# Moving output-projection halves around each context tile, summing the last blocks in PSUM, and reordering the loads and the start of an attention-times-FFN kernel

## The chip, the cores and the metric

The kernel runs on one core of one Trainium2 chip. Times are device microseconds of that core. Unless a profile is named, a time is the median of four to seven executions. Engines are called by their usual short names: PE is TensorE, DVE is VectorE, ACT is ScalarE, POOL is GpSimd, and SP is SyncE, which here only issues DMAs.

## The reference

With x of shape 2048 x 640 and 32 heads of 192 columns, cut to what matters:

```python
xn = layernorm(x)
k, v = k_cache[:, :, 1536:], v_cache[:, :, 1536:]      # the last 512 keys only
p  = softmax((xn @ wq) @ k.T * 192 ** -0.5)            # per head
s  = (p @ v, heads side by side) @ wo                  # 6144 -> 640
g  = silu((silu(xn @ w_gate) * (xn @ w_up)) @ w_down)
out = x + s * g
```

## The kernel before

The kernel has a head (layer norm and feed-forward, giving g), then 64 attention steps: 16 pairs of heads by 4 blocks of 512 queries. Step `i` computes the scores of `i`, the query projection of `i+1`, the context (`pv`) of `i-1` and the output projection (`wo_half`) of `i-3`. Everything is issued in program order on every engine. The result of `wo_half` is added on DVE to `sacc`, in SBUF, for 16 tiles of 128 queries. DVE also prepares the keys of the next pair: it sums them (the K sums) and subtracts their mean. Two PSUM accumulators named `mm` serve both the query chunks and the output halves. The cuts are marked with "...".

```python
def mm_tile():                                   # two buffers for q chunks and output halves
    return psum.tile([P, 512], f32, name="mm", tag="mm", bufs=2)

def q_chunk(i, j):
    q_ps = mm_tile()
    ...                                          # 5 matmuls of 512 columns
    nc.scalar.copy(qTs[i][:, j, :], q_ps[:, :])  # ACT frees the buffer

def wo_half(i, qt, n):
    ps = mm_tile()
    ...                                          # 3 matmuls of 320 columns
    nc.vector.tensor_tensor(sacc[:, t, cols], sacc[:, t, cols], ps[:, 0:HD], ALU.add)
    if pr == NPAIR - 2 and n == 1:
        pre_final(t)                             # POOL: sacc = sacc * g2 + x
    ...                                          # last pair: DVE or ACT+POOL make ob, SP stores it

order = ("A", 0, 1, "q0", 2, 3, "B", 4, "q1", 5, 6, "q2", 7)
for step in order:                               # A, B: scores; q: query chunk
    ...
        wo_half(i - LAG, step // 2, step % 2)    # one half, then one context half
        pv(i - 1, step // 2, step % 2)
        prepare_pair(i, step)                    # loads, K transposes, K sums of the next pair
```

In the head all gate, up and down weights are issued before the x tiles 4 to 7, all on SP except the first quarter of the up weights, which ACT issues.

The softmax here doesn't subtract the row's maximum and nothing guards it: scores larger than these inputs give would overflow.

## Time and profile before

| | before |
|---|---|
| median of the first four runs | 1005.62 us |
| span of the profiled run | 1003.2 us |
| PE busy | 974.6 us (97%) |
| start to first exponential of step 0 | 185.2 us |
| from there to first exponential of step 63 | 772.5 us |
| from there to the end | 45.5 us |

The last three rows come from the starts of ACT's exponentials in the timeline. They split the span into head, steady part and tail. A PE that is 97% busy can still be losing time: the profile draws each group of matmuls to its modelled end, which overlaps the start of the next group, so short holes show only as a late start of the next one. Therefore look at starts.

From the page of the kernel before: the span, PE's busy time, and the clock granted to TensorE in 40 slices (tenths of full speed).

```profile
span 1003.2 us, 16007 instructions
...
PE 974.6 (97%) x6540; PEld 564.7 (56%) x6540; DVE 522.7 (52%) x1265; ACT 421.1 (42%) x561; POOL 151.5 (15%) x188
...
PEclk8999999999999999999999999999999999999979
```

**Steady.** From the timeline of the kernel before, PE alone (start, duration, engine, line, operation, output and inputs, count; in brackets, where there are any, the idle time before and what ended it), and DVE alone and one line of ACT in the same stretch:

```profile
504.77 0.50 PE L373 MATMUL pv<-V_b_210,p_t 128*128 128x193 bf16 x4
505.20 0.57 PE L412 MATMUL mm<-wo_p,OT_b 128*128 128x320 bf16 x3
...
505.94 1.24 PE L158 MATMUL mm<-xnT,wq_p 128*128 128x512 bf16 x5
507.17 0.57 PE L412 MATMUL mm<-wo_p,OT_b 128*128 128x320 bf16 x3
...
507.91 1.02 PE L347 MATMUL sc<-qT,khat 128*128 128x512 bf16 x4
...
520.33 1.03 PE L347 MATMUL sc<-qT,khat 128*128 128x512 bf16 x4
```

```profile
506.05 0.68 DVE L140 TENSOR_REDUCE ssum<-KT 128x1 f32<-128x512 bf16 x1
506.64 0.48 DVE L419 TENSOR_TENSOR sacc<-sacc,mm 128x320 f32<-128x320 f32 x1
```

```profile
504.56 0.59 ACT L163 CAST qT<-mm 128x512 bf16<-128x512 f32 x1
```

Four context matmuls (pv) take 0.33 us from start to next start elsewhere, but the output half after those at 504.77 starts 0.43 us later, at 505.20, just when ACT's eviction of the query chunk has ended (504.56 to 505.15). The half at 507.17 starts 1.23 us after the query chunk at 505.94, which takes 1.07 us where nothing is in the way. It starts 50 ns after the add at 506.64 ends, and that add stood behind a K sum. The two score groups (L347) at 507.91 and 520.33 begin two steps.

A step takes 12.42 us, and 12.57 us in the third block of each pair, where the K sums are.

**Head.** The same view, around the wait for x tile 4:

```profile
23.21 0.89 DVE L207 BATCH_NORM_STATS2 stats<-x_t 128x6 f32<-128x320 bf16 x2 [5.82 <-DMA x_t<-in_A_x_dram]
24.13 0.21 DVE L208 BATCH_NORM_AGGREGATE mv<-stats 128x2 f32<-128x12 f32 x1
24.26 0.64 DVE L257 TENSOR_TENSOR hT<-sc,sg 128x512 bf16<-128x512 f32 x1
...
24.95 2.29 PE L251 MATMUL sc<-xnT,wg_sb 128*128 128x512 bf16 x5 [4.60 <-DVE hT L257]
```

DVE works in order. The statistics of x tile 4 wait for a load queued behind all weights, the product hT is behind them, and PE waits for hT. The five matmuls at 24.95 then take 2.29 us where they take 1.24 us at full clock.

**Tail.** Who PE waited for after 955 us (total, times, longest), from the timeline two output additions on DVE with POOL's work beside the first, and the line of the windows view for 970 to 980 us (busy time and count by engine, then the granted clock, the DMA share and GB/s):

```profile
PE mm L412 <- DVE s_f L431: 11.1, 15, 1.7
```

```profile
959.80 1.41 POOL L403 TENSOR_TENSOR sacc<-sacc,g_76 128x640 f32<-128x640 f32 x1
...
960.04 1.53 DVE L432 TENSOR_TENSOR ob<-s_f,sacc 128x320 bf16<-128x320 f32 x1
...
976.29 0.49 DVE L432 TENSOR_TENSOR ob<-s_f,sacc 128x320 bf16<-128x320 f32 x1
```

```profile
970.00:980.00 10.00, 7.98 (x42) 5.37 (x42) 9.52 (x20) 0.00 (x0) 4.72 (x4) 0.59 0.41 105
```

The same addition took 1.53 us beside POOL's multiplication and 0.49 us alone. The Trainium skill, page "SBUF — State Buffer", section "SBUF: two separate sides", says that a DVE operation with two SBUF inputs and a GpSimd operation that reads SBUF exclude each other on a shared pair of ports, each for a whole instruction. The trace agrees: the slow addition ends 0.36 us after POOL's multiplication (961.57 and 961.21). In the window from 970 to 980 us PE was also granted only 0.59 of full speed.

### The profile page before, as it was taken

Reading aid. Unit: us, or ns where it says so; the run is one execution under the profiler, and the core shown is the slowest. Engines: PE = TensorE matmul, PEld = TensorE weight load, DVE = VectorE, ACT = ScalarE, POOL = GpSimd, SP = SyncE. Lnnn points to the kernel's source line nnn. Section 1 sums busy time; section 2 is a strip of 40 time slices with the busy share of each in tenths; the row PEclk is TensorE's granted clock in tenths of the full one; section 3 lists DMA queues with packets and bytes.
Section 4 is the critical chain, followed back from the end, with each engine's and each line's share of the span. In section 5 each row is a group of like instructions: output and inputs, shape, how many; then the busy total and the mean of one; then the engine's idle time right before and its main releaser. Section 6 shows DMA issues by size and latency. Waiting matters only on the chain. (4 is left out here: it accounts for less than half of the span.)

```text
span 1003.2 us, 16007 instructions
## 1 busy us (share of the span) xinstructions
PE 974.6 (97%) x6540; PEld 564.7 (56%) x6540; DVE 522.7 (52%) x1265; ACT 421.1 (42%) x561; POOL 151.5 (15%) x188
## 2 busy tenths in 40 slices
PE   6999999999999999999999999999999999999974
PEld 2455555555555555555555555555555555555553
DVE  3443411155555565656555655555555555556585
ACT  2332322554444444444444444444444444444421
POOL 1020400000101010101010101010101010005875
PEclk8999999999999999999999999999999999999979
DMA  9040800033533333324333423343433233222332
GB/s 301 27 99 2 157 17 1 1 59 73 87 64 87 64 88 64 88 63 87 65 87 63 88 63 88 64 87 64 87 64 88 63 87 65 58 49 55 74 97 73
DMA packets 145593, 74.18 MB, mean 74 GB/s; under 512 B 127856, under 2 KB 138608, under 8 KB 145520
## 3 DMA queue, kind: packets, MB, share of 16 engines
q1 hardware_dynamic: 135872, 41.40, 20.8%
q0 software_dynamic: 8704, 30.94, 12.1%
q8 instruction: 51, 0.84, 0.3%
q10 hardware_dynamic: 944, 0.82, 0.3%
q14 instruction: 22, 0.18, 0.1%
HBM read 39.45 MB, written 2.62 MB: 42 GB/s over the span
## 5 line engine op out<-in xcount | busy, mean ns | idle before, releaser
L419 DVE TENSOR_TENSOR sacc<-sacc,mm 128x320 f32<-128x320 f32 x448 | 217.6, 486 | 294.4 <-PE mm L412 291.7
L360 ACT ACTIVATE p_t<-sc 128x1024 bf16<-128x1024 f32 x256 | 248.1, 1020 | 229.9 <-PE sc L355 229.8
L412 PE MATMUL mm<-wo_p,OT_b 128*128 128x320 bf16 x1536 | 293.9, 301 | 11.5 <-DVE s_f L431 11.1
L158 PE MATMUL mm<-xnT,wq_p 128*128 128x512 bf16 x960 | 238.2, 379 | 0.0
L412 PEld LDWEIGHTS <-OT_b 128*128 128x128 bf16 x1536 | 139.0, 97 | 144.9 <-issue 69.8
L373 PEld LDWEIGHTS <-p_t 128*128 128x128 bf16 x2048 | 186.1, 98 | 42.1 <-issue 1.7
L163 ACT CAST qT<-mm 128x512 bf16<-128x512 f32 x192 | 112.3, 585 | 192.9 <-PE mm L158 184.4
L382 DVE TENSOR_TENSOR O_b<-pv,r 128x384 bf16<-128x384 f32 x256 | 142.7, 557 | 8.8
L347 PE MATMUL sc<-qT,khat 128*128 128x512 bf16 x512 | 131.8, 379 | 1.1 <-ACT qT L163 0.9
L158 PEld LDWEIGHTS <-wq_p 128*128 128x128 bf16 x960 | 90.7, 97 | 69.3 <-issue 0.8
L373 PE MATMUL pv<-V_b_210,p_t 128*128 128x193 bf16 x768 | 96.2, 249 | 0.0
L257 DVE TENSOR_TENSOR hT<-sc,sg 128x512 bf16<-128x512 f32 x48 | 33.1, 689 | 96.1 <-ACT sg L256 96.1
L373 PE MATMUL pv<-V_b_214,p_t 128*128 128x193 bf16 x640 | 79.5, 246 | 0.0
L373 PE MATMUL pv<-V_b_212,p_t 128*128 128x193 bf16 x640 | 79.5, 246 | 0.0
L355 PE MATMUL sc<-qT,khat 64*128 64x512 bf16 x512 | 77.5, 381 | 0.0
L251 PE MATMUL sc<-xnT,wg_sb 128*128 128x512 bf16 x240 | 61.6, 389 | 5.4 <-DVE hT L257 4.6
L347 PEld LDWEIGHTS <-khat 128*128 128x128 bf16 x512 | 48.1, 97 | 32.4 <-issue 2.0
L256 ACT ACTIVATE sg<-sc 128x512 bf16<-128x512 f32 x48 | 28.7, 597 | 86.4 <-PE sc L251 86.4
L251 PE MATMUL sc<-xnT,wu_sb 128*128 128x512 bf16 x240 | 61.6, 389 | 0.0
L381 DVE RECIPROCAL r<-pv 128x2 f32<-128x2 f32 x256 | 41.5, 162 | 34.9 <-PE pv L373 34.9
L119 POOL DMA_DIRECT2D wo_p<-in_A_wo_dram x16 | 12.3, 769 | 310.8 <-PE mm L412 310.8
L265 PE MATMUL mm<-wd_sb,hT 128*128 128x320 bf16 x384 | 56.6, 299 | 0.0
(55 smaller groups left out, 423.6 us busy)
## 6 DMA issues: line engine op xcount, KB each, us to landing
wq_p<-in_A_wq_dram POOLq DMA_DIRECT2D x16, 480.0 KB, 7.0
wo_p<-in_A_wo_dram POOLq DMA_DIRECT2D x16, 480.0 KB, 4.4
K_p<-in_A_k_cache_dram POOLq DMA_DIRECT2D x32, 192.0 KB, 4.3
x_r<-in_A_x_dram POOLq DMA_DIRECT2D x16, 160.0 KB, 2.6
out_dram<-ob SPq DMA_DIRECT2D x16, 160.0 KB, 1.8
V_b_210<-in_A_v_cache_dram POOLq DMA_DIRECT2D x12, 192.0 KB, 3.1
x_t<-in_A_x_dram SPq DMA_DIRECT2D x14, 160.0 KB, 4.1
wg_sb<-in_B_w_gate_dram SPq DMA_DIRECT2D x4, 480.0 KB, 8.3
```

The source lines that it names most:

```text
L158: nc.tensor.matmul(q_ps[:, :], pairs[pr]["wq"][:, c, j * P : (j + 1) * P], xnT[:, c, b * 512 : (b + 1) * 512], start=(c == 0), stop=(c == ...
L163: nc.scalar.copy(qTs[i][:, j, :], q_ps[:, :])
L251: nc.tensor.matmul(gu[:, s, :], w_sb[:, c, f * P : (f + 1) * P], xnT[:, c, qc], start=(c == 0), stop=(c == NC - 1),)
L265: nc.tensor.matmul(dn[:, 0:HD], hTs[b][:, f, ti * P : (ti + 1) * P], wd_sb[:, f, cols], start=(f == 0), stop=(f == NF - 1),)
L347: nc.tensor.matmul(sc[:, h, :], khat[:, 2 * h, ks], qT[:, 2 * h, :], start=True, stop=False)
L355: nc.tensor.matmul(sc[:, h, :], khat[r, 1, ks], qT[r, 1, :], start=False, stop=True)
L360: nc.scalar.activation(p_t[:, :, :], sc[:, :, :], ACT.Exp, scale=scale)
L373: nc.tensor.matmul(acc[:, h, 0 : Dh + 1], Ps[i][kc][:, h, qt * P : (qt + 1) * P], V_p[:, kc, h, 0 : Dh + 1], start=(kc == 0), stop=(kc == ...
L381: nc.vector.reciprocal(r[:], acc[:, :, Dh : Dh + 1])
L382: nc.vector.tensor_tensor(Obs[i][:, qt, :, :], acc[:, :, 0:Dh], r[:].to_broadcast([P, 2, Dh]), ALU.mult)
L412: nc.tensor.matmul(ps[:, 0:HD], OTs[i][:, 3 * qt + j, :], pairs[pr]["wo"][:, j, cols], start=(j == 0), stop=(j == 2),)
L419: nc.vector.tensor_tensor(sacc[:, t, cols], sacc[:, t, cols], ps[:, 0:HD], ALU.add)
```

## The change

The intent is threefold. In the steady part, the two output halves of a tile stand around both context halves, so that an `mm` buffer has time to come free. In the head, x tiles 4 to 7 are loaded between the weights and PE is kept busy. In the tail, blocks 2 and 3 of the last two pairs are summed in PSUM at the end, and the output of those tiles is made by DVE alone; POOL's multiply-and-add for them comes earlier, after pair 13 (pairs count from 0), and for the tiles of blocks 0 and 1 it now comes last. Some buffer counts change too. The diff, cut to its core:

```diff
 # head
-load all of w_gate, w_up, w_down, then x tiles 4-7
+load w_gate/w_up quarters 0, 1; x tiles 4-7; quarters 2, 3; w_down
+keep_warm(13) ... keep_warm(9) ... keep_warm(1) ...     # matmuls on zeros between the transposes
-if nx and f < 4: ln_stats(...)
+if nx and 2 <= f < 6: ln_stats(...)
-ln_apply partly on ACT
+ln_apply on DVE throughout
 # steady
-order = ("A", 0, 1, "q0", 2, 3, "B", 4, "q1", 5, 6, "q2", 7)
+order = ("A", 0, "q0", 1, "B", 2, "q1", "q2", 3)
-wo_half(i - LAG, step // 2, step % 2); pv(i - 1, step // 2, step % 2)
+wo_half(o, step, 0); pv(i - 1, step, 0); pv(i - 1, step, 1); wo_half(o, step, 1)
-K sums at context halves 1, 3, 5
+K sums at "q0", "B", "q1"
 # tail
+def load_xr(t):
+    xrs[t] = finp.tile([P, D], bf, name="x_r", bufs=4)
+    nc.sync.dma_start(out=xrs[t][:], in_=x2[t * P : (t + 1) * P, :])       # was on nc.gpsimd
+def gate_and_add(t, dst):                                                # POOL, two operations
+    nc.gpsimd.tensor_tensor(sacc[:, t, :], sacc[:, t, :], g2[:, t, :], ALU.mult)
+    nc.gpsimd.tensor_tensor(dst, sacc[:, t, :], xrs.pop(t)[:], ALU.add)
+def store(t, ob):
+    nc.sync.dma_start(out=out2[t * P : (t + 1) * P, :], in_=ob[:])
+wo_half, last pair, blocks 0 and 1: n == 0: load_xr(t); n == 1: gate_and_add(t, ob), store(t, ob)
+wo_late(b, qt): 12 matmuls of pairs 14 and 15 into PSUM; DVE: s_f = ps * g2, ob = s_f + sacc; store
+the last context blocks are transposed by DMA on nc.sync, one tile of 128 queries at a time
+the very last block is scaled on ACT (was DVE); PE transposes it, as before
```

## The prediction

> **What bounds the kernel.** TensorE (PE): the page gives a span of 1003.2 us with PE busy 974.6 us (97%). By the starts of matmuls in the timeline, a 512-column matmul takes a slot of 213 ns, a 320-column one 133, a 193-column one 80, and two 64-row score matmuls share a slot. All columns at that rate are an estimated 900 us. The other 103 us are gaps; the change is about three groups of them.
>
> 1. *Steady attention* (58 of 64 steps of pair and query block). A step takes 12.42 us, 12.57 us in the one of four with K's sums, for 11.53 us of columns. The timeline shows about 0.3 us of holes per step before output halves (16.1 us between 220 and 900 us): there are two "mm" accumulators, and a half waits for the 585 ns query eviction on ScalarE, or for the 486 ns sacc add behind a 675 ns K sum on VectorE. Another 0.3 us per step stands around the 64-row matmuls.
> 2. *Head.* PE idles 4.6 us at 20.4-25.0 us: VectorE, in order, stands at the statistics of x tile 4, whose load is behind all weights (landing at 23.2 us). Matmuls at 12.0-15.6 and 25.0-29.2 us have twice the spacing (427 ns). PE loses 9.0 us between 12 and 40 us.
> 3. *Tail.* After 960 us there are 17.6 us of columns and 18.7 us of gaps: output halves wait for VectorE's s_f/ob (0.48 + up to 1.53 us while GpSimd runs), later for GpSimd's s_f/ob, 1.8 us per tile (chain of waits). The granted clock (windows view) falls to 0.59 at 970-980 us.
>
> **What the change does, costed.**
> - Steady: the output halves stand around both context halves (0.67 us), so the half after a query chunk comes 1.07 us after it; eviction takes 0.8. The tight spot becomes reciprocal, 557 ns O_b scaling, then sacc add: the buffer is free 2.15 us after the context tile starts, and PE wants it at 2.145. Nearly no hole, no margin. K's sums move to slack. Expect 12.15 us per step: minus 16 us.
> - Head: x tiles 4-7 come after half of the weights, statistics start two hidden blocks later; extra zero matmuls keep the clock up. The Trainium skill ("TensorE: Matmul & The Clock Gate", Part 1) says the clock halves after an idle window of about 3.4 us and needs as long to return; the doubled spacings agree. Hidden blocks start near 11.3 instead of 12.03 us, at full rate: minus 9.3 us.
> - Tail: 8 tiles of the last two pairs accumulate in PSUM, without GpSimd or ScalarE in the output; a 640-column pair of VectorE operations (estimated 1.7 us from 486 ns per 320) faces 1.6 to 2.4 us of PE per tile. Gaps fall from 18.7 to about 2.5 us, the end after the last matmul from 6.9 to 6.2: minus 17 us.
>
> PE is critical throughout, so the parts add: minus 42 us, span 961.5 us, time **963.5 us**, 80% range **956 to 972**. Faster by over 2%: 0.97; within 2%: 0.025; slower: 0.005.
>
> **What would show it.** Steps of 12.1 to 12.2 us, the same for all four blocks; no PE gap over 1 us after 12 us; no granted clock under 0.95 after the first hidden block; 427 ns spacing only in the first zero matmuls; after the last step about 17 us of dense PE work, GpSimd's gate-and-add (2.8 us per tile) finishing under it.
>
> **What would make it wrong.** The sacc wait showing 0.1 us twice per step (+10 us); weights landing later than hidden blocks need them; the in-order SyncE queue holding the last transposes behind stores that wait for GpSimd; VectorE's ob slowed by GpSimd (1.53 against 0.49 us).

## The result

The changed kernel took 972.42 us (972.38 to 973.19, four runs) against 1005.62 us before. The ratio is 0.9671, with a 95% interval of 0.9654 to 0.9688. A ratio is the mean time of one kernel's runs over that of the other's of the same rounds, so not quite the ratio of the medians. It is faster by 3.3%, but the gain is 33 us and not 42, and 972.42 is just outside the predicted 956 to 972.

From the page after, the same lines:

```profile
span 970.6 us, 15644 instructions
...
PE 945.9 (97%) x6449; PEld 561.5 (58%) x6550; DVE 507.5 (52%) x1233; ACT 419.7 (43%) x559; POOL 127.5 (13%) x152
...
PEclk9999999999999999999999999999999999999999
```

Some matmul records are missing (6449 of 6550), so groups below sometimes count one short.

**Steady after**, from the timeline, PE alone and DVE alone:

```profile
503.59 1.03 PE L355 MATMUL sc<-qT,khat 128*128 128x512 bf16 x4
...
506.17 0.57 PE L438 MATMUL mm<-wo_p,OT_b 128*128 128x320 bf16 x3
506.58 1.24 PE L158 MATMUL mm<-xnT,wq_p 128*128 128x512 bf16 x4
507.66 0.57 PE L438 MATMUL mm<-wo_p,OT_b 128*128 128x320 bf16 x3
...
515.77 1.03 PE L355 MATMUL sc<-qT,khat 128*128 128x512 bf16 x3
```

```profile
506.58 0.56 DVE L392 TENSOR_TENSOR O_b<-pv,r 128x384 bf16<-128x384 f32 x1
507.05 0.48 DVE L456 TENSOR_TENSOR sacc<-sacc,mm 128x320 f32<-128x320 f32 x1
```

The add that frees the buffer ends at 507.53 and the next half starts at 507.66, 1.08 us after the query chunk began, so there is no hole. The step, from the score group at 503.59 to that at 515.77, takes 12.18 us, the median in all four blocks.

**Head after.** The hidden blocks start at 11.09 us at full clock, and the statistics of x tile 4 wait for nothing:

```profile
11.09 1.24 PE L254 MATMUL sc<-xnT,wg_sb 128*128 128x512 bf16 x4 [0.24 <-DVE xnT L245]
...
19.00 0.87 DVE L218 BATCH_NORM_STATS2 stats<-x_t 128x6 f32<-128x320 bf16 x2
```

**Tail after.** Here is what had not been expected. Who PE waited for after 925 us:

```profile
PE pv L381 <- ACT O_b L397: 4.9, 2, 3.1
PE sc L438 <- DMA OT_b<-O_b: 3.5, 2, 1.8
PE trp L416 <- ACT O_b L397: 1.5, 1, 1.5
PE mm L438 <- DMA OT_b<-O_b: 0.6, 1, 0.6
```

These waits sum to 10.5 us. PE waited for transposed context tiles (OT_b), and for ACT's scaling of the last block, which waited for a reciprocal on DVE. DVE, in turn, stood before that reciprocal at an addition whose output buffer `ob` was not yet stored:

```profile
DVE ob L485 <- DMA out_dram<-ob: 7.6, 2, 4.8
```

SP's and POOL's timelines in the same stretch:

```profile
937.55 0.34 SPq L428 DMA_DIRECT2D out_dram<-ob  x1
937.94 0.42 SPq L421 DMA_DIRECT2D x_r<-in_A_x_dram  x1
938.47 1.18 SPq L401 DMA_TRANSPOSE OT_b<-O_b  x1
941.79 0.34 SPq L428 DMA_DIRECT2D out_dram<-ob  x1
```

```profile
931.67 1.40 POOL L425 TENSOR_TENSOR ob<-sacc,x_r 128x640 bf16<-128x640 f32 x1 [2.71 <-DMA x_r<-in_A_x_dram]
...
937.48 1.40 POOL L424 TENSOR_TENSOR sacc<-sacc,g_76 128x640 f32<-128x640 f32 x1
940.37 1.40 POOL L425 TENSOR_TENSOR ob<-sacc,x_r 128x640 bf16<-128x640 f32 x1 [1.49 <-issue]
```

Read them as one circle. The store at 941.79 waits for POOL's addition, which runs from 940.37 to 941.77. That addition waits for the x_r load issued at 937.94. The load was issued only after the store of the tile before, at 937.55, and that store had waited for POOL's previous addition. The profile itself names the load as what ended the wait only at 926.20 and 931.67; at 940.37 it prints "issue", which names nothing. That the load is the cause there too is shown by e1 and e4 below, which change only the loads. So one tile takes 4.2 us here and 4.57 us on average (the first addition starts at 921.70 and the eighth at 953.72, seven periods), where POOL's own work is 2.8 us. The context transpose at 938.47 is in the same queue, and it too is held to this beat.

The parts of the span, from ACT's exponentials in the timelines (us):

| | to step 0 | steps 0 to 63 | step 63 to end | time |
|---|---|---|---|---|
| before | 185.2 | 772.5 | 45.5 | 1005.6 |
| after | 175.7 | 754.0 | 40.8 | 972.4 |

Step 61 of the changed kernel has no output halves and takes 8.92 us instead of 12.18; those 3.3 us of work are done in the tail. With them put back, the spans say: head 9.5 us, steady 15.2, tail 7.9 us saved, 32.6 in all.

### The profile page after: what moved, and what is told of

It reads as the page before. It is cut to its first block, busy times and chain, and to the rows that moved or that the text cites. A ratio compares the mean times of both kernels' runs of the same rounds, so it can differ in the third digit from the quotient of the medians.

```text
span 970.6 us, 15644 instructions
## 1 busy us (share of the span) xinstructions
PE 945.9 (97%) x6449; PEld 561.5 (58%) x6550; DVE 507.5 (52%) x1233; ACT 419.7 (43%) x559; POOL 127.5 (13%) x152
## 3 DMA queue, kind: packets, MB, share of 16 engines
q0 software_dynamic: 7936, 28.32, 11.3%
## 4 chain that ended last, share of the span: by engine, by line
PE 91%; DMA 2%; issue 2%; DVE 2%; POOL 1%; SPq 0%; ACT 0%; POOLq 0%; DVEq 0%
PE mm L158 21%; PE mm L438 21%; PE pv L381 17%; PE sc L355 11%; PE sc L254 10%; PE sc L363 7%; PE mm L268 5%; DMA x_r<-in_A_x_dram 1%; POOL ob L425 1%; DMA KT<-K_p 0%; PE tp L240 0%; DVE stats L218 0%; DVE s_f L482 0%; DMA out_dram<-ob 0%; DMA x_t<-in_A_x_dram 0%
## 5 line engine op out<-in xcount | busy, mean ns | idle before, releaser
L438 PE MATMUL mm<-wo_p,OT_b 128*128 128x320 bf16 x1452 | 276.6, 300 | 1.3 <-DVE sacc L456 0.7
L158 PE MATMUL mm<-xnT,wq_p 128*128 128x512 bf16 x915 | 225.7, 379 | 2.8 <-DVE sacc L456 0.4
L438 PEld LDWEIGHTS <-OT_b 128*128 128x128 bf16 x1536 | 136.2, 97 | 106.4 <-issue 51.9
L381 PEld LDWEIGHTS <-p_t 128*128 128x128 bf16 x2048 | 177.8, 97 | 27.5 <-issue 3.9
L158 PEld LDWEIGHTS <-wq_p 128*128 128x128 bf16 x960 | 93.7, 98 | 93.4 <-issue 1.5
L392 DVE TENSOR_TENSOR O_b<-pv,r 128x384 bf16<-128x384 f32 x252 | 140.5, 558 | 8.8 <-DVE r L390 0.3
L355 PE MATMUL sc<-qT,khat 128*128 128x512 bf16 x472 | 129.4, 379 | 3.0 <-ACT qT L163 0.9
L381 PE MATMUL pv<-V_b_222,p_t 128*128 128x193 bf16 x768 | 79.8, 246 | 4.9 <-ACT O_b L397 4.9
L381 PE MATMUL pv<-V_b_226,p_t 128*128 128x193 bf16 x640 | 66.5, 246 | 0.0
L381 PE MATMUL pv<-V_b_224,p_t 128*128 128x193 bf16 x640 | 66.5, 246 | 0.0
L254 PE MATMUL sc<-xnT,wg_sb 128*128 128x512 bf16 x230 | 59.1, 379 | 0.8 <-DVE xnT L245 0.2
L254 PE MATMUL sc<-xnT,wu_sb 128*128 128x512 bf16 x234 | 58.5, 379 | 0.2
```

The lines of the kernel that those rows point to most:

```text
L158: nc.tensor.matmul(q_ps[:, :], pairs[pr]["wq"][:, c, j * P : (j + 1) * P], xnT[:, c, b * 512 : (b + 1) * 512], start=(c == 0), stop=(c == ...
L254: nc.tensor.matmul(gu[:, s, :], w_sb[:, c, f * P : (f + 1) * P], xnT[:, c, qc], start=(c == 0), stop=(c == NC - 1),)
L355: nc.tensor.matmul(sc[:, h, :], khat[:, 2 * h, ks], qT[:, 2 * h, :], start=True, stop=False)
L381: nc.tensor.matmul(acc[:, h, 0 : Dh + 1], Ps[i][kc][:, h, qt * P : (qt + 1) * P], V_p[:, kc, h, 0 : Dh + 1], start=(kc == 0), stop=(kc == ...
L392: nc.vector.tensor_tensor(O_b[:, qt, :, :], acc[:, :, 0:Dh], r[:].to_broadcast([P, 2, Dh]), ALU.mult)
L438: nc.tensor.matmul(ps, OTs[i][:, 3 * qt + j, :], pairs[i // NB]["wo"][:, j, cols], start=(first and j == 0), stop=(last and j == 2),)
```

## The experiments

Three theories went into the first round. The ring theory says that the missing gain is the circle just shown. Rival 1 says that POOL's eight tiles are simply too much work for the shortened last steps. Rival 2 says that three `ob` buffers are too few. Two further runs ask whether the head and the order have the gains credited to them. All kernels gave correct results.

### e1_xr_act: the x_r loads on another queue

```diff
-nc.sync.dma_start(out=xrs[t][:], in_=x2[...])
+nc.scalar.dma_start(out=xrs[t][:], in_=x2[...])
```

> One line differs from the changed kernel: the loads of x for the final addition (x_r) are issued by ScalarE's queue instead of SyncE's. Ring theory (the changed kernel's tail is slow because, on the in-order SyncE queue, the x_r load of a tile stands behind the store of the tile before, that store waits for GpSimd's addition, and GpSimd's addition waits for the x_r load, so GpSimd goes at 4.4 us per tile and holds the context transposes and stores behind it): the loads land early, GpSimd goes at 2.8 us per tile, PE's waits for OT_b after 935 us vanish, time 963 to 966 us against 972.4. Rival 1 (GpSimd's 8 gate-and-add tiles are simply too much work for the last two steps): within 1 us of 972.4. Rival 2 (three ob buffers are too few): 970 or more.

Measured: 963.87 us (963.57 to 964.55), ratio to the kernel before 0.9595. POOL's additions now follow each other in 3.06 us on average (922.68 to 944.11, seven periods; 2.8 had been expected). PE's waits after 925 us:

```profile
PE trp L416 <- ACT O_b L397: 1.1, 1, 1.1
PE pv L381 <- ACT O_b L397: 0.4, 1, 0.4
```

No wait for OT_b is left. Rival 1 falls: POOL's work is the same and 8.5 us are back. What remains of a buffer shortage is one DVE wait of 2.8 us for an `ob` buffer.

### e2_ob8: more output buffers alone

```diff
-ob = finp.tile([P, D], bf, name="ob")
+ob = finp.tile([P, D], bf, name="ob", bufs=8)
```

> The changed kernel with 8 output buffers (ob) instead of 3, nothing else. Ring theory: PE's three waits for OT_b (0.6, 1.8 and 1.7 us) stay and two more come in their place; only VectorE's waits for an ob buffer go; GpSimd keeps 4.4 us per tile; time 969 to 971.5 us. Rival 2 (buffers are the cause): 963 to 966 us. Rival 1 (GpSimd's work): about 972.

Measured: 971.43 us (971.02 to 974.0), ratio 0.9675, so no different from the changed kernel at 0.9671, and within what the ring theory expected. PE's waits after 925 us:

```profile
PE sc L438 <- DMA OT_b<-O_b: 6.9, 4, 2.1
PE mm L438 <- DMA OT_b<-O_b: 1.0, 1, 1.0
```

The waits behind DVE went, and waits for the transposes took their place: five, as expected. POOL's additions came no faster than before (4.83 us apart on average). Rival 2 falls as the main cause. The buffer waits were a second effect of the same late stores, lying in the shadow of the late transposes.

### e4_xr_early: the same queue, loads four tiles ahead

```diff
+if i == NS - LAG:                       # the step without output halves
+    for t in range(4): load_xr(t)
 # wo_half, last pair, after store(t, ob):
+    if b == 0: load_xr(t + 4)
-if n == 0 and (pre or final): load_xr(t)
+if n == 0 and pre: load_xr(t)
```

> The changed kernel with the x_r loads still on SyncE's queue, but issued four tiles ahead (the first four in the step without output halves, each of the others after the store of the tile four before). Ring theory: the ring is broken though the queue is the same: GpSimd at 2.8 us per tile, 963 to 966 us, as with the loads on ScalarE's queue (963.9). If instead it was the load on SyncE's queue as such (a load between two transposes delaying them): 970 or more.

Measured: 962.74 us (962.62 to 963.1), ratio 0.9575, a little under the expected 963 to 966. The loads stay on SP, and the circle is cut by their place in the queue alone. POOL's timeline:

```profile
935.70 1.40 POOL L424 TENSOR_TENSOR sacc<-sacc,g 128x640 f32<-128x640 f32 x1
937.18 1.40 POOL L425 TENSOR_TENSOR ob<-sacc,x_r 128x640 bf16<-128x640 f32 x1
```

There is no bracket before the addition: the load has long landed. PE's waits after 925 us fall from 10.5 to 1.0 us (0.6 and 0.4, both for ACT).

### e3_store_pool: POOL issues the stores of its own tiles

```diff
-store(t, ob)                            # SP
+store(t, ob, nc.gpsimd)                 # for the eight gate-and-add tiles
```

> The changed kernel with the stores of the eight gate-and-add tiles issued by GpSimd itself; x_r loads and transposes stay on SyncE as they were. Ring theory: SyncE no longer waits for GpSimd except for an x_r buffer four tiles back, so loads and transposes go early; GpSimd pays about 0.6 us more per tile for issuing (3.4 us per tile): 964 to 967 us. If the three ob buffers or GpSimd's work were the cause: 971 or more.

Measured: 968.09 us (967.72 to 968.24), ratio 0.9627. The expectation of 964 to 967 was missed. SP's loads and transposes did go early, with no PE wait for OT_b, but POOL went at 3.80 us per tile and not 3.4, and one wait of another kind was left. POOL's timeline, then PE's only wait after 925 us, then DVE's:

```profile
936.85 1.40 POOL L425 TENSOR_TENSOR ob<-sacc,x_r 128x640 bf16<-128x640 f32 x1
938.55 0.58 POOL L428 DMA_DIRECT2D out_dram<-ob  x1 [0.30 <-POOL ob L425]
```

```profile
PE pv L381 <- ACT O_b L397: 5.2, 1, 5.2
```

```profile
DVE ob L485 <- DMA out_dram<-ob: 5.0, 2, 4.0
```

Issuing a store costs POOL 0.58 us and another 0.30 us until it sees its own addition done. At that pace the third `ob` buffer does come back too late, and PE waits behind DVE. After that wait the granted clock was 0.50 from 945 to 950 us (windows view), so this miss has a second part that the waits do not show.

### e6_store_pool_ob8: the same with eight buffers

> GpSimd issues the stores of its eight tiles (968.1 us, a miss: 964 to 967 was expected), now with 8 ob buffers. Its profile shows GpSimd at 3.8 us per tile and one PE wait of 5.2 us behind VectorE, which waits 4.0 us for an ob buffer. If that buffer wait is the whole of the miss: 962.5 to 964.5 us and no PE wait over 1 us in the tail. If GpSimd's slower pace costs otherwise: 966 or more.

Measured: 963.29 us (963.26 to 963.71), ratio 0.9586, as expected from the buffer wait. One PE wait of 1.4 us stayed, where none over 1 us had been expected. So the miss of the run before was the buffers (with the clock lost in the wait they caused). Whether they matter depends on how late the stores are.

### p_order and p_head: parts of the change on the kernel before

p_order is the kernel before with the new order of the step and the new places in it for K's loads, transposes, sums and centring, and nothing else. p_head is the kernel before with the new head alone.

```diff
 # p_order
-order = ("A", 0, 1, "q0", 2, 3, "B", 4, "q1", 5, 6, "q2", 7)
+order = ("A", 0, "q0", 1, "B", 2, "q1", "q2", 3)   # wo_half, pv, pv, wo_half in each tile
 # p_head
-head of the kernel before
+head of the changed kernel
```

> The kernel before with the order of the step alone: output halves around both context halves, chunks q1 and q2 together, K's sums beside the chunks; head and tail as before. If the two output halves' waits for the mm accumulators are the 0.3 us holes: steps of 12.18 us in all four blocks, about 14 us less than before, 990 to 993 us. If instead the shorter steps of the changed kernel come from another part of it (buffer counts, fewer GpSimd and DMA issues), steps stay near 12.42 us.

> The kernel before with the head of the changed one alone (x tiles 4-7 between the weights, later statistics, zero matmuls, VectorE for all normalisations). If the head's gain is its own: first exponential at 175.7 us as in the changed kernel (185.2 before), 9 to 10 us less than before, 995.5 to 997 us, steps of 12.42 and 12.57 us unchanged.

Measured: p_order 989.99 us (988.62 to 991.59), ratio 0.9855; p_head 996.43 us (996.38 to 996.52), ratio 0.9918. p_order's steps take 12.18 us, and its part from step 0 to 63 is 755.9 us against 772.5. p_head reaches step 0 at 175.9 us against 185.2, and its steps keep 12.42 and 12.57 us. Both 95% intervals lie below 1 (0.9837 to 0.9872, and 0.9901 to 0.9935). Each part brings its own gain; p_order does not touch the head, nor p_head the steps.

### p_head_order: the changed kernel without its tail

```diff
-tail of the changed kernel
+tail of the kernel before, with the new head and the new order
```

> The changed kernel without its tail: the kernel before with the new head and the new step order. If the parts add: 1005.6 - 9.2 - 15.6 = 981 us, so that the tail as it is brings 8 to 9 us (predicted 17), and with the ring broken 17. If head and order interact, this run differs from 981 by more than 2 us.

Measured: 980.48 us (980.08 to 981.08), ratio 0.9751. The parts add within 2 us: against the kernel before in their own rounds (1004.95 us) they bring 15.0 and 8.5 us, and together, against 1005.64 us, 25.2. (The expected 981 us had mixed rounds.) From here to the changed kernel are 8.1 us, and to e4_xr_early 17.7 us: that is what this tail brings with the ring and without it.

### e5_xr_act_ob8 and e7_best: both repairs

```diff
+e5: x_r loads on ACT's queue, ob bufs=8
+e7: x_r loads four tiles ahead on SP, ob bufs=8
```

> Both: x_r loads on ScalarE's queue and 8 ob buffers. With the ring gone the profile still shows VectorE waiting 2.8 us for an ob buffer and PE 1.5 us behind it. If that wait is real: 962 to 963 us; if GpSimd's stores still pace the end: 963.9 as without the buffers.

> x_r loads four tiles ahead on SyncE and 8 ob buffers: the two repairs that each took waits out of the tail. VectorE still waited 2.3 us for an ob buffer with the early loads alone, PE some 0.6 us behind it. Expected 961.5 to 962.7 us against 962.7 without the buffers; if the buffers do nothing here, 962.7 within 0.3.

Measured: e5 963.04 us (962.82 to 963.19), ratio 0.9577, just above what was expected. e7 took 961.93 us (961.71 to 962.06), ratio 0.9573 (0.9558 to 0.9587). Its only PE wait after 925 us:

```profile
PE pv L381 <- ACT O_b L397: 0.4, 1, 0.4
```

e7 beats both kernels. It is 0.8 us under e4 by the medians, but the two ran in different rounds, and by the ratios (0.9575 and 0.9573) the difference is 0.2 us. One wait of 0.6 us vanished from the profile; a gain from the buffers here is not shown by the times.

The spans of all runs, from ACT's exponentials (us):

| | to step 0 | steps 0 to 63 | step 63 to end |
|---|---|---|---|
| before | 185.2 | 772.5 | 45.5 |
| p_head | 175.9 | 772.5 | 46.3 |
| p_order | 185.7 | 755.9 | 46.7 |
| p_head_order | 175.9 | 756.9 | 45.6 |
| after | 175.7 | 754.0 | 40.8 |
| e2_ob8 | 175.8 | 754.1 | 39.8 |
| e3_store_pool | 175.9 | 753.8 | 36.7 |
| e6_store_pool_ob8 | 175.9 | 754.5 | 31.5 |
| e1_xr_act | 176.0 | 754.8 | 31.2 |
| e4_xr_early | 175.9 | 754.2 | 30.8 |
| e5_xr_act_ob8 | 175.9 | 755.0 | 30.3 |
| e7_best | 176.1 | 753.8 | 30.0 |

Only the last column moves among the variants of the tail. The middle column varies by about 1 us even where nothing in it was changed. In the changed kernel one step of 13.53 us accounts for 1.35 us: a K transpose issued at 676.32 landed 4.58 us later, where the median is 2.7 us, and DVE stood behind it. It is step 42, and in the profiles that same step takes 13.3 to 13.6 us in all nine runs that have both the new head and the new order, and 12.2 to 12.6 us in the other three (e1 and e5 have one more, step 58, of 13.1 and 13.2 us). So it is not random: it comes with the two parts together, costs about 1.4 us, and neither part shows it alone; why this transpose lands late was not pursued.

## Why the prediction was wrong

The direction, the steady part and the head were right. The step that failed is one term of the sum.

- *Steady, minus 16 us.* Right: 15.2 us by the spans (16.6 in p_order, which has no late step 42), 12.18 us per step in all four blocks (predicted 12.15, "12.1 to 12.2"). The feared 0.1 us twice per step did not come. The add starts 1.55 us after the context tile (505.50 to 507.05) where 1.62 had been estimated (2.15 less the add and its signal), and so ends 0.13 us before PE starts the next half.
- *K's sums.* Right that they cease to cost: the third block takes 12.18 us like the others. That it is their new place, and not the new place of the adds alone, was not tried separately. In the kernel before, one sum stood directly in front of an add whose buffer PE needed next. Now a query chunk or a score group comes in between.
- *Head, minus 9.3 us.* Right: 9.5 us by the spans, and p_head alone gives 8.5 us of time in its own rounds. Hidden blocks start at 11.09 us, against 11.3 predicted.
- *Tail, minus 17 us.* Wrong as the kernel stands: 7.9 us by the spans, 8.1 by the step from p_head_order. The failed term is "Gaps fall from 18.7 to about 2.5 us". PE's waits alone were 10.5 us, of which 6.4 stood behind DVE's late reciprocals (gone in e2, with eight output buffers) and 4.1 behind late transposes. The failed assumption under it is "GpSimd's gate-and-add (2.8 us per tile) finishing under it": it took 4.57 us per tile. The prediction listed "the in-order SyncE queue holding the last transposes behind stores that wait for GpSimd" as a danger and gave it no time. It did not mention that the x_r loads had been moved into that same queue, which turns the danger from a delay into a circle. The arithmetic had taken POOL's busy time per tile for its period. Summing the circle from the durations would have given it away: store issue 0.4, load to landing about 2.5 (2.6 on the page before), addition 1.4, together 4.3 us.
- *The rest of the tail was right.* With the circle cut, the same tail brings 17.7 us, and the kernel takes 962.7 to 963.9 us where 963.5 was predicted. DVE's pair of operations per late tile (0.82 and 0.83 us, predicted 1.7 together) is no bottleneck.
- *"No PE gap over 1 us after 12 us"*: wrong in the tail (3.1, 1.8 and 1.5 us, among others), and this sign pointed to the failed step. *"No granted clock under 0.95"*: right for the 40 slices of the page (by the windows view 1.00, and 0.96 in the last), though 0.82 in the last 5.6 us, when PE had run out of work.

That a wait in the circle is spent on the issuing queue is also what the Trainium skill states, on the page "DMA: Bandwidth & Descriptors", section "Anatomy of one DMA — SWDGE (gpsimd) path": "DMA engines do not wait on semaphores — any semaphore wait happens on the issuing sequencer before dispatch". The section is about DMAs issued by GpSimd. The trace agrees for SP: the store at 941.79 was issued 0.02 us after POOL's addition ended, and the load behind it at 942.19.

## What to carry to other kernels

When a load, a store and a compute engine are tied to one in-order queue, write down for each instruction in that queue what it waits for; if following the waits leads back to the queue, the period is the sum around the circle and not the longest busy time. Put loads that need nothing ahead of stores that wait, by prefetch distance or by another queue, and judge buffer counts only after that. A moved line such as the issuing engine of a small load can cost a quarter of what a large rewrite gains.

## What the Trainium skill lacked or had wrong

- "DMA: Bandwidth & Descriptors" says that semaphore waits happen on the issuing sequencer, but that page does not draw the consequence that a waiting store holds back every later load and transpose of its queue. Here that made 4.57 us per tile out of 2.8 and cost 8.5 to 9.7 us, recovered by moving the loads (e1_xr_act, e4_xr_early). "Perfetto Trace Analysis", section "DMA Optimizations", comes nearest, with the advice to issue loads and stores from different engines; it gives neither this reason nor a cost.
- The same page's section "Issuing engines are not separate DMA queues" says that issuing from several engines "will only save the time on the sequencer it takes to initiate the DMA, which is usually small relative to the DMA itself". Moving the sixteen x_r loads (160 KB each) from SP to ACT saved 8.5 us, because it also moved them out of the shadow of another DMA's wait; e4_xr_early saved 9.7 us without changing the issuing engine.
- No page that was consulted gives the time that GpSimd loses by issuing a store of its own result: 0.58 us for the instruction and 0.30 us of waiting before it (e3_store_pool).
- "TensorE: Matmul & The Clock Gate", section "HAM oscillation — how this bites in real kernels", gives the rule of no idle gap over about 3.4 us. In the tail of the kernel before, the granted clock fell to 0.59 between 970 and 980 us although PE's longest wait in the tail was 1.7 us. The page's next section tells of short idle times that halve the clock, but gives no figure for how busy a window must be; between 960 and 970 us PE was busy for 6.67 of 10 us. The runs yield no such figure either: in the changed kernel PE was busy for only 7.3 of the 15 us from 940 to 955 us, with a wait of 3.1 us, and the clock stayed at 1.00; in e2_ob8, whose longest wait was 2.1 us, it was 0.66 from 950 to 955 us.
